# A gated recurrence and its feed-forward block: one masked product per chunk in place of seven levels, with the old algorithm kept behind a branch

## The chip, the core and the metric

The kernel runs on one core of a Trainium2 chip. The metric is the device time of one execution in microseconds (us). Of the core's engines, PE (TensorE) multiplies matrices, DVE (VectorE), ACT (ScalarE) and POOL (GpSimd) work element by element, and SP (SyncE) issues transfers. Each engine runs its own queue in order and waits on semaphores of the others.

## What is computed

Inputs are q, k, v, a_re, a_im of shape (4, 8, 768, 48) in float32 (batch, heads, steps, head size) and two weight matrices, 384 x 2048 and 2048 x 384, which arrive as float64. a_re lies between 0.85 and 0.95, a_im is normal with deviation 0.1. Cut to what matters:

```python
mag = np.sqrt(a_re * a_re + a_im * a_im)
scale = np.minimum(mag, 0.999) / (mag + 1e-06)
for t in range(S):
    new_re = ar * S_re - ai * S_im          # ar, ai: scaled gates of step t
    new_im = ar * S_im + ai * S_re
    S_re, S_im = new_re + kv, new_im        # kv: outer product of k[t] and v[t]
    y[:, :, t] = einsum('bhd,bhde->bhe', q[:, :, t], S_re)
h = x @ w_in                                # x: y as 3072 tokens of 384
sp = np.maximum(h, 0.0) + np.log1p(np.exp(-np.abs(h)))
out = (h * erf(sp)) @ w_out
```

## The kernel before, in words

The tokens are split into NU = 12 units of 256 steps, each of C = 2 chunks of 128 steps; three units follow one another in a batch element and hand on a state. Heads go in NHG = 2 groups of HG = 4. A complex gate is a decay r and an angle. The running sum of the angles turns queries and keys by cosine and sine, which leaves a real recurrence with decay r over 2 x 48 = 96 rows.

*Gates of a unit.* `gate_decay` (from L221) makes r with squares, a logarithm and an exponential on ACT, and some fifteen DVE passes over 768 columns, among them a reciprocal (L267) and r itself in two copies (L278). `gate_angle` (L292, L293, L305 to L311) takes the arc tangent, sums angles over a chunk with a triangular matmul (L305), adds the carry of the chunk before with a second one (L307), and takes sines.

*A chunk* (`attention`). For a head group r, k and q are transposed on PE (L340) and copied out by ACT (L347, L354, L361). A product of keys and queries gives the diagonal (L370, masked on DVE at L373). Seven levels follow, for blocks of m = 1, 2, ..., 64 steps:

```python
nc.tensor.matmul(out=lv[:, j], lhsT=K[0:D2, j, :], rhs=Qv[0:D2, j, :, 1, :], ...)        # L384
nc.vector.copy_predicated(out=halves(A, 1), mask=pair[l], data=lv...)                     # L389
nc.vector.tensor_tensor(out=halves(Q, 1)[0:D2], ..., in1=over(0), op=OP.mult)             # L398
nc.gpsimd.tensor_tensor(out=halves(K, 0)[0:D2], ..., in1=over(1), op=OP.mult)             # L400
nc.vector.tensor_tensor(out=nt[0:D2], in0=tv[:, :, 0], in1=tv[:, :, 1], op=OP.mult)       # L402
```

Each level's matmuls need the K and Q that the level before scaled. Then y is A times v plus Q times the carried state (L411, L414), and the state takes in the scaled keys, transposed back (L424), times v (L429, L436, L437). `to_xT` (L448) transposes y for the projections.

*Feed-forward of a unit.* Two slabs of 1024 hidden columns. `ff_in` projects (L475), and copies h on ACT (L477) and a clipped h on DVE (L480). `softplus` makes four ACT passes over 2048 columns (L146 is the helper of every table function, L145 its table load). `erf_times_h` has four parts of a slab, each with two DVE passes, a Gelu on ACT and two DVE passes more (L505 to L509). `ff_out` projects back with 16 accumulating products for each 128 tokens (L519) and writes (L522, L524). A float32 matmul appears in the profile as two instructions.

*Order.* `weave` emits the steps of several streams evenly over parts of a window. In window u run the recurrence of unit u over the whole window, the gates of unit u + 1, and the feed-forward of unit u - 1 over the first 0.85. Window 0 has the 14 steps that narrow the weights to float32 instead (`narrow`, L175: six DVE passes and two POOL products each, ending at L198), which use the buffers of h and z. Transfers are issued by SP.

## Time and profile before

| what | value |
|---|---|
| median of 3 runs | 1558.09 us (1557.83 to 1559.02) |
| profiled execution, its span from first to last instruction | 1557.6 us |
| instructions | 18736, of them 6912 matmuls |
| busy: PE, DVE, ACT, POOL | 1350.9, 1171.2, 597.6, 418.0 us |

The profile shows one execution. Only its span is given for it; it is the time between its first and last instruction, and it stands 0.5 us under the median of the runs. Busy time is the union of an engine's instructions. Idle time of an engine that does not set the pace costs nothing. The granted clock is the share of 2.4 GHz at which PE is allowed to run; 0.5 is 1.2 GHz.

### The profile page before, as it was taken

The page shows a single profiled execution, that of the slowest core. Times are in us where ns is not written, and L with a number is a line of the kernel's source. Part 1 is how long each engine was busy: PE and PEld are TensorE (multiplying, and loading weights), DVE is VectorE, ACT ScalarE, POOL GpSimd, SP SyncE. Part 2 cuts the span into 40 slices and gives each one's busy share as a digit, 9 for nine tenths or more (in the row PEclk, how much of TensorE's full clock was granted, in tenths as well). Part 3 has the DMA queues.
Part 4 walks back from the last instruction along what each step waited for, and adds up shares of the span by engine and source line. Part 5 has one row for each costly group of instructions (what it writes and reads, how often), then busy time and mean ns, then how long its engine had stood idle before and what let it go on. Part 6 is the DMA issues. An engine that isn't in the chain of part 4 may idle for free.

```text
span 1557.6 us, 18736 instructions
## 1 busy us (share of the span) xinstructions
PE 1350.9 (87%) x6912; PEld 1137.9 (73%) x6912; DVE 1171.2 (75%) x2104; ACT 597.6 (38%) x751; POOL 418.0 (27%) x387
## 2 busy tenths in 40 slices
PE   0455598998998998998998998998998998999997
PEld 0244477887877787787877787887877887888784
DVE  6999979579579669579589669579589669578535
ACT  2301033443443443444443443434443443434425
POOL 4445523122123222122132222122132122132210
PEclk9997557797797886797797887797797887799888
DMA  8214100100100100100100100100100100000000
GB/s 173 90 31 114 58 11 11 31 21 11 32 21 11 31 21 11 31 21 11 32 21 11 31 21 11 31 21 11 31 21 10 31 21 0 1 11 1 0 11 10
DMA packets 131386, 42.09 MB, mean 27 GB/s; under 512 B 125408, under 2 KB 128480, under 8 KB 130528
## 3 DMA queue, kind: packets, MB, share of 16 engines
q1 hardware_dynamic: 131296, 40.90, 11.4%
q8 instruction: 55, 0.90, 0.2%
q14 instruction: 35, 0.29, 0.1%
HBM read 36.18 MB, written 4.72 MB: 26 GB/s over the span
## 4 chain that ended last, share of the span: by engine, by line
PE 60%; DVE 25%; issue 6%; ACT 6%; POOL 2%; DMA 0%; SPq 0%; DVEq 0%; ACTq 0%; POOLq 0%
PE lv L384 20%; PE ops L519 12%; PE hps L475 9%; PE y L411 4%; DVE y L267 3%; PE y L414 3%; PE tr L340 3%; PE kv L429 3%; ACT z L146 2%; DVE A L389 2%; PE dg L370 2%; DVE tot L402 2%; DVE z L480 2%; DVE Q L398 1%; POOL K L400 1%
## 5 line engine op out<-in xcount | busy, mean ns | idle before, releaser
L384 PEld LDWEIGHTS lv<-Q,K 96*128 96x128 f32 x2688 | 438.3, 246 | 158.9 <-issue 100.6
L384 PE MATMUL lv<-Q,K 96*128 96x64 f32 x2688 | 448.6, 330 | 101.5 <-DVE Q L398 90.7
L400 POOL TENSOR_TENSOR K<-K,tot 96x256 f32<-96x256 f32 x280 | 262.7, 939 | 377.0 <-PE lv L384 243.8
L475 PE MATMUL hps<-xT,w_in_sb 128*128 128x256 f32 x1152 | 305.5, 415 | 0.6 <-ACT xT L449 0.6
L519 PE MATMUL ops<-w_out_sb,h 128*128 128x384 f32 x768 | 283.6, 498 | 7.8 <-DVE z L480 6.5
L146 ACT ACTIVATE z<-z 128x2048 f32<-128x2048 f32 (+1 forms) x144 | 152.3, 1057 | 319.9 <-DVE t L505 308.6
L475 PEld LDWEIGHTS hps<-xT,w_in_sb 128*128 128x128 f32 x1152 | 232.8, 212 | 32.2 <-ACT xT L449 1.0
L400 POOL TENSOR_TENSOR K<-K,rT 96x256 f32<-96x256 f32 x48 | 74.1, 1544 | 640.5 <-PE lv L384 640.5
L389 DVE COPY_PREDICATED A<-pair,lv 128x256 f32<-128x256 uint8 x336 | 171.3, 510 | 42.1 <-PE lv L384 39.4
L519 PEld LDWEIGHTS ops<-w_out_sb,h 128*128 128x128 f32 x768 | 135.1, 192 | 71.1 <-DVE z L480 6.9
L398 DVE TENSOR_TENSOR Q<-Q,tot 96x256 f32<-96x256 f32 x280 | 150.2, 536 | 0.0
L477 ACT COPY h<-hps 128x512 f32<-128x512 f32 x96 | 55.8, 581 | 161.0 <-PE hps L475 161.0
L437 DVE TENSOR_TENSOR S<-S,kv 96x192 f32<-96x192 f32 x32 | 11.2, 350 | 133.1 <-PE kv L429 133.1
L480 DVE TENSOR_SCALAR z<-hps 128x512 f32<-128x512 f32 x96 | 65.0, 682 | 44.1 <-ACT h L477 44.1
L411 PE MATMUL y<-v,A 128*128 128x48 f32 x384 | 95.3, 354 | 0.2 <-DVE tot L402 0.2
L411 PEld LDWEIGHTS y<-v,A 128*128 128x128 f32 x384 | 84.3, 279 | 0.4 <-DVE tot L402 0.4
L426 ACT COPY kn<-kn 128x384 f32<-128x384 f32 x40 | 19.2, 479 | 165.6 <-PE kn L424 146.3
L340 PE MATMUL tr<-ident,r 128*96 128x128 f32 x192 | 49.5, 387 | 37.3 <-DVE r L278 36.5
L414 PE MATMUL y<-S,Q 96*128 96x48 f32 x320 | 81.4, 347 | 0.0
L145 ACT ACT_TABLE_LOAD x62 | 79.5, 1283 | 1.1
L505 DVE TENSOR_TENSOR t<-z,yy 128x512 f32<-128x512 f32 x96 | 71.7, 747 | 9.7 <-ACT yy L146 9.7
L506 DVE SCALAR_TENSOR_TENSOR yy<-t,yy 128x512 f32<-128x512 f32 x96 | 74.7, 778 | 0.1
(96 smaller groups left out, 1753.6 us busy)
## 6 DMA issues: line engine op xcount, KB each, us to landing
raw<-in_moe_w_in_dram SPq DMA_DIRECT2D x6, 1024.0 KB, 5.5
raw<-in_moe_w_out_dram SPq DMA_DIRECT2D x8, 768.0 KB, 4.3
ar<-in_a_re_dram SPq DMA_DIRECT2D x24, 192.0 KB, 3.2
ai<-in_a_im_dram SPq DMA_DIRECT2D x24, 192.0 KB, 3.2
q<-in_q_dram SPq DMA_DIRECT2D x24, 192.0 KB, 3.7
k<-in_k_dram SPq DMA_DIRECT2D x24, 192.0 KB, 3.3
v<-in_v_dram SPq DMA_DIRECT2D x24, 192.0 KB, 3.2
out_dram<-o SPq DMA_DIRECT2D x24, 192.0 KB, 1.9
```

The costliest lines, as they stand in the source:

```text
L145: in_order(nc.scalar.preload_act_table_set(sets[0]))
L146: in_order(nc.scalar.activation(func=func, **kw))
L340: nc.tensor.transpose(out=ps[0:D2, j, :], in_=src(j), identity=ident)
L384: nc.tensor.matmul(out=lv[:, j], lhsT=K[0:D2, j, :], rhs=Qv[0:D2, j, :, 1, :], start=True, stop=True)
L389: nc.vector.copy_predicated(out=halves(A, 1), mask=pair[l], data=lv.rearrange("p h b m -> p (h b) m"))
L398: nc.vector.tensor_tensor(out=halves(Q, 1)[0:D2], in0=halves(Q, 1)[0:D2], in1=over(0), op=OP.mult)
L400: nc.gpsimd.tensor_tensor(out=halves(K, 0)[0:D2], in0=halves(K, 0)[0:D2], in1=over(1), op=OP.mult)
L411: nc.tensor.matmul(out=y[:, j, :], lhsT=st["A"][:, j, :], rhs=T["v", u][:, c, hg * HG + j, :], start=True, stop=first)
L414: nc.tensor.matmul(out=y[:, j, :], lhsT=st["Q"][0:D2, j, :], rhs=T["S", hg][0:D2, j, :], start=False, stop=True)
L475: nc.tensor.matmul(out=ps[:, e, :], lhsT=w_in_sb[:, kd, f0:f0 + P], rhs=T["xT", u][:, kd, :], start=(kd == 0), stop=(kd == KD - 1))
L480: nc.vector.tensor_scalar(out=T["z", u, sl][:, i:i + 2, :], in0=ps, scalar1=8.0, scalar2=-16.0, op0=OP.min, op1=OP.max)
L519: nc.tensor.matmul(out=ps, lhsT=T["h", u, sl][:, e, jj * P:(jj + 1) * P], rhs=w_out_sb[:, i, :], start=(i == 0), stop=(i == KF - 1))
```

## The change

`quotient_path` is new; the old kernel stays, word for word, as `product_path`. With c the running sum of the logarithms of the decays in a chunk, a query is scaled by exp(c) and a key by exp(-c) before they are turned and transposed. One product of keys and queries per head, masked by the upper triangle, then stands for the diagonal and all levels. The state is the old state plus keys times values, times the decays of the whole chunk, which a transfer through memory brings from a row into columns. Keys need no second transposition.

The gates: a slope ai/ar from a reciprocal of ar, clipped to 1.5, and its arc tangent; the log decay from the squares; four of the gate products and one product per erf part are on POOL. The carry of the angle is a row that a transfer brings to the first step's row. The clip of h reads SBUF, not PSUM. The windows run from -2 to 13: gates up to three units ahead, recurrence of w, first projection and erf of w - 1, second projection of w - 2 in eight pieces. The narrowing is in windows -1 (w_in) and 0 (w_out), with one words buffer where there were two. At the end two sums (of exp(-c), limit 1e13, and of the excess of the slope over 1.5, limit 0) are tested, the answer is loaded into a register, and if it is 0 the old algorithm runs over the same output.

```diff
+def quotient_path(
...
+    ldq = ctx.enter_context(tc.tile_pool(name="ldq", bufs=1))
...
+    hp = ctx.enter_context(tc.tile_pool(name="hp", bufs=4))
+    zp = ctx.enter_context(tc.tile_pool(name="zp", bufs=1))
...
+    def g_tan(u):
+        ar, ai = flat(T["ar", u]), flat(T["ai", u])
+        def s0():
+            s, y, m = t_("s"), t_("y"), t_("m")
+            act(out=s, in_=ar, func=AF.Square)
+            act(out=y, in_=ai, func=AF.Square)
+            nc.gpsimd.tensor_tensor(out=s, in0=s, in1=y, op=OP.add)
+            act(out=m, in_=ai, func=AF.Abs, scale=1.0 / SLOPE)
+            nc.gpsimd.tensor_tensor(out=m, in0=m, in1=ar, op=OP.subtract)
+            act(out=m, in_=m, func=AF.Relu, accum_out=off[:, u:u + 1])
+            T["s"], T["y"] = s, y
+        def s1():
+            rec = t_("rec")
+            nc.vector.tensor_scalar(out=rec, in0=ar, scalar1=2.0**-60, scalar2=None, op0=OP.max)
+            nc.vector.reciprocal(out=rec, in_=rec)
+            T["rec"] = rec
+        def s2():
+            rec = T["rec"]
+            nc.gpsimd.tensor_tensor(out=rec, in0=rec, in1=ai, op=OP.mult)
+            s = T["s"]
+            nc.vector.tensor_scalar(out=s, in0=s, scalar1=2.0**-63, scalar2=2.0**63, op0=OP.max, op1=OP.min)
+            th = gat.tile([P, C, DM], FP, tag="th", name="th")
+            nc.vector.tensor_scalar(out=th.rearrange("p c f -> p (c f)"), in0=rec, scalar1=SLOPE, scalar2=-SLOPE,
+                                    op0=OP.min, op1=OP.max)
+            T["th", u] = th
+        return [s0, s1, s2]
+    def g_turn(u):
+        return [lambda: act(out=T["th", u], in_=T["th", u], func=AF.Arctan)]
+    def g_angle(u):
+        def run(c):
+            def f():
+                th = T["th", u][:, c, :]
+                if u % PER > 0 or c > 0:
+                    prev = T["F", u][:, c - 1, :] if c > 0 else T["F", u - 1][:, C - 1, :]
+                    row = att1.tile([1, DM], FP, tag="row", name="row")
+                    nc.sync.dma_start(out=row, in_=prev[P - 1:P, :])
+                    nc.vector.scalar_tensor_tensor(out=th[0:1, :], in0=row, scalar=TAU, in1=th[0:1, :],
+                                                   op0=OP.mult, op1=OP.add)
+                ps = ps_b.tile([P, DM], FP, tag="b", name="sum")
+                nc.tensor.matmul(out=ps, lhsT=turns, rhs=th, start=True, stop=True)
+                if c == 0:
+                    T["F", u] = gat.tile([P, C, DM], FP, tag="F", name="F")
+                F = T["F", u][:, c, :]
+                w = att1.tile([P, DM], FP, tag="part", name="whole", bufs=2)
+                nc.vector.tensor_scalar(out=w, in0=ps, scalar1=MAGIC, scalar2=MAGIC, op0=OP.add, op1=OP.subtract)
+                nc.vector.tensor_tensor(out=F, in0=ps, in1=w, op=OP.subtract)
+            return f
+        return [run(c) for c in range(C)]
+    def g_sin(u):
+        def f():
+            F, CS, n = T["F", u], gat.tile([P, C, 2, DM], FP, tag="CS", name="CS", bufs=2), t_("n")
+            n = n.rearrange("p (c f) -> p c f", c=C)
+            act(out=n, in_=F, func=AF.Abs)
+            act(out=CS[:, :, 0, :], in_=n, func=AF.Sin, scale=-TAU, bias=half_pi)
+            act(out=CS[:, :, 1, :], in_=F, func=AF.Sin, scale=TAU)
+            T["CS", u] = CS
+        return [f]
+    def g_log(u):
+        def f():
+            s, y = T["s"], T["y"]
+            lr = gat.tile([P, C, DM], FP, tag="lr", name="lr")
+            act(out=s, in_=s, func=AF.Ln)
+            act(out=y, in_=s, func=AF.Exp, scale=-0.5)
+            act(out=y, in_=y, func=AF.Ln, scale=EPS, bias=1.0)
+            nc.vector.tensor_scalar(out=s, in0=s, scalar1=0.5, scalar2=math.log(CAP), op0=OP.mult, op1=OP.min)
+            nc.gpsimd.tensor_tensor(out=lr.rearrange("p c f -> p (c f)"), in0=s, in1=y, op=OP.subtract)
+            T["lr", u] = lr
+        return [f]
+    def g_decay(u):
+        def run(c):
+            def f():
+                if c == 0:
+                    T["pr", u] = gat.tile([P, C, 2, DM], FP, tag="pr", name="pr", bufs=2)
+                pr = T["pr", u]
+                ps = ps_b.tile([P, DM], FP, tag="b", name="sum")
+                nc.tensor.matmul(out=ps, lhsT=triu, rhs=T["lr", u][:, c, :], start=True, stop=True)
+                act(out=pr[:, c, 0, :], in_=ps, func=AF.Exp)
+                i = u * C + c
+                act(out=pr[:, c, 1, :], in_=ps, func=AF.Exp, scale=-1.0, accum_out=spans[:, i:i + 1])
+                s = u % PER
+                if s * C + c < PER * C - 1:
+                    w = att2.tile([P, H], FP, tag=f"w{c}", name="w")
+                    row = dram.tile([H, D], FP, tag="row", name="wrow")
+                    nc.sync.dma_start(out=row, in_=pr[P - 1:P, c, 0, :].rearrange("p (h d) -> p h d", d=D))
+                    with nc.allow_non_contiguous_dma(reason="a row into a column"):
+                        for e in range(2):
+                            nc.sync.dma_start(out=w[e * D:(e + 1) * D, :], in_=row.rearrange("h d -> d h"))
+                    T["w", u, c] = w
+            return f
+        return [run(c) for c in range(C)]
+    def chunk(u, c):
+        s = u % PER
+        first = s == 0 and c == 0
+        last = s == PER - 1 and c == C - 1
+        st = {}
+        def prep(nm, e):
+            def f():
+                a = att1.tile([P, H, D], FP, tag="part", name=nm + "r", bufs=2)
+                nc.vector.tensor_tensor(out=a, in0=T[nm, u][:, c], op=OP.mult,
+                                        in1=T["pr", u][:, c, e, :].rearrange("p (h d) -> p h d", d=D))
+                t = att1.tile([P, H, 2, D], FP, tag=nm + "t", name=nm + "t")
+                cs = T["CS", u][:, c].rearrange("p u (h d) -> p h u d", d=D)
+                nc.vector.tensor_tensor(out=t, in0=a.unsqueeze(2).to_broadcast([P, H, 2, D]), in1=cs, op=OP.mult)
+                st[nm] = t
+            return f
+        def cols(nm, g):
+            def f():
+                ps = ps_a.tile([P, HG, P], FP, tag="a", name="tr")
+                for j in range(HG):
+                    nc.tensor.transpose(out=ps[0:D2, j, :], in_=st[nm][:, g * HG + j].rearrange("p u d -> p (u d)"),
+                                        identity=ident)
+                t = att2.tile([P, HG, P], FP, tag=f"{nm}T", name=f"{nm}T", bufs=2 if nm == "k" else 3)
+                nc.scalar.copy(out=t[0:D2], in_=ps[0:D2])
+                st[nm, g] = t
+            return f
+        def scores(g):
+            def f():
+                ps = ps_a.tile([P, HG, P], FP, tag="a", name="sc")
+                for j in range(HG):
+                    nc.tensor.matmul(out=ps[:, j, :], lhsT=st["k", g][0:D2, j, :], rhs=st["q", g][0:D2, j, :],
+                                     start=True, stop=True)
+                A = att2.tile([P, HG, P], FP, tag="A", name="A")
+                nc.vector.tensor_tensor(out=A, in0=ps, in1=triu.unsqueeze(1).to_broadcast([P, HG, P]), op=OP.mult)
+                st["A", g] = A
+            return f
+        def state():
+            if last:
+                return
+            kv = ps_b.tile([P, H, D], FP, tag="b", name="kv")
+            for j in range(H):
+                nc.tensor.matmul(out=kv[0:D2, j, :], lhsT=st["k"][:, j].rearrange("p u d -> p (u d)"),
+                                 rhs=T["v", u][:, c, j, :], start=True, stop=True)
+            ns = att2.tile([P, H, D], FP, tag="S", name="S")
+            w = T["w", u, c][0:D2].unsqueeze(2).to_broadcast([D2, H, D])
+            if first:
+                nc.vector.tensor_tensor(out=ns[0:D2], in0=kv[0:D2], in1=w, op=OP.mult)
+            else:
+                t = att1.tile([P, H, D], FP, tag="part", name="Skv", bufs=2)
+                nc.vector.tensor_tensor(out=t[0:D2], in0=kv[0:D2], in1=T["S"][0:D2], op=OP.add)
+                nc.vector.tensor_tensor(out=ns[0:D2], in0=t[0:D2], in1=w, op=OP.mult)
+            st["S"] = ns
+        def y_():
+            y = ps_b.tile([P, H, D], FP, tag="b", name="y")
+            for j in range(H):
+                g, i = divmod(j, HG)
+                nc.tensor.matmul(out=y[:, j, :], lhsT=st["A", g][:, i, :], rhs=T["v", u][:, c, j, :],
+                                 start=True, stop=first)
+                if not first:
+                    nc.tensor.matmul(out=y[:, j, :], lhsT=st["q", g][0:D2, i, :], rhs=T["S"][0:D2, j, :],
+                                     start=False, stop=True)
+            if not last:
+                T["S"] = st["S"]
+            x = xp.tile([P, DM], FP, tag="x", name="x")
+            nc.scalar.copy(out=x, in_=y.rearrange("p h d -> p (h d)"))
+            st["x"] = x
...
+        return [prep("k", 1), prep("q", 0), cols("k", 0), cols("k", 1), cols("q", 0), scores(0), cols("q", 1),
+                scores(1), state, y_, xT]
...
+    def softplus(u, sl):
+        half = SLAB // 2
+        def f():
+            h = T["h", u, sl]
+            z = zp.tile([P, SLAB, NT], FP, tag="z", name="z")
+            y = yp.tile([P, SLAB, NT], FP, tag="yy", name="yy")
+            for i in range(0, SLAB, half):
+                nc.vector.tensor_scalar(out=z[:, i:i + half], in0=h[:, i:i + half], scalar1=8.0, scalar2=-16.0,
+                                        op0=OP.min, op1=OP.max)
+            act(out=z, in_=z, func=AF.Exp)
...
+                t = yp.tile([P, n, NT], FP, tag="t", name="t", bufs=2)
+                nc.gpsimd.tensor_tensor(out=t, in0=z, in1=y, op=OP.mult)
...
+    def ff_out(u):
+        n = 4
+        def piece(i0, jj):
+            def f():
+                if i0 == 0:
+                    T["o", u, jj] = ps_o.tile([P, DM], FP, tag="o", name="ops")
+                ps = T["o", u, jj]
+                for i in range(i0, i0 + n):
+                    sl, e = divmod(i, SLAB)
+                    nc.tensor.matmul(out=ps, lhsT=T["h", u, sl][:, e, jj * P:(jj + 1) * P], rhs=w_out_sb[:, i, :],
+                                     start=(i == 0), stop=(i == KF - 1))
+                if i0 + n == KF:
+                    o = op.tile([P, DM], FP, tag="o", name="o")
+                    nc.scalar.mul(out=o, in_=ps, mul=-RT2)
+                    t0 = (u * C + jj) * P
+                    nc.sync.dma_start(out=out[t0:t0 + P, :], in_=o)
+            return f
+        return [piece(i0, jj) for i0 in range(0, KF, n) for jj in range(C)]
+    load_gates(0)
+    load_gates(1)
+    load_qkv(0)
+    for f in g_tan(0):
+        f()
+    for w in range(-2, NU + 2):
+        load_gates(w + 4)
+        if w >= -1:
+            load_qkv(w + 2)
+        rec = chunk(w, 0) + chunk(w, 1) if 0 <= w < NU else []
+        f0 = only(w - 1, lambda u: ff_in(u, 0) + softplus(u, 0) + erf_times_h(u, 0))
+        f1 = only(w - 1, lambda u: ff_in(u, 1) + softplus(u, 1) + erf_times_h(u, 1))
+        wts = weights_in() if w == -1 else weights_out() if w == 0 else []
+        weave(
+            (0.0, 1.0, rec),
+            (0.0, 0.05, only(w + 2, g_turn) + only(w + 1, g_sin)),
+            (0.0, 0.9, wts),
+            (0.0, 0.45, f0), (0.45, 0.9, f1),
+            (0.2, 1.0, only(w - 2, ff_out)),
+            (0.3, 0.7, only(w + 2, g_angle)),
+            (0.15, 0.151, only(w + 1, g_decay) + only(w + 2, g_log)),
+            (0.5, 0.8, only(w + 3, g_tan)),
+        )
...
+    nc.tensor.matmul(out=ps[0:1, :], lhsT=ones, rhs=total, start=True, stop=True)
...
+    nc.vector.tensor_scalar(out=both[:, 0:1], in0=ps[0:1, 0:1], scalar1=SPAN, scalar2=None, op0=OP.is_le)
+    nc.vector.tensor_scalar(out=both[:, 1:2], in0=ps[0:1, 1:2], scalar1=0.0, scalar2=None, op0=OP.is_le)
+    nc.vector.tensor_tensor(out=ok, in0=both[:, 0:1], in1=both[:, 1:2], op=OP.mult)
...
+    with tc.tile_pool(name="ok", bufs=1) as pool:
+        ok = pool.tile([1, 1], I32, name="ok")
+        quotient_path(tc, q, k, v, a_re, a_im, w_in, w_out, out, ok)
+        fine = nc.values_load(ok[0:1, 0:1], min_val=0, max_val=1)
+        with tc.If(fine < 1):
+            product_path(tc, q, k, v, a_re, a_im, w_in, w_out, out)
```

## Rows read from the trace of the kernel before

**Rows 1.** The page: span, busy time by engine, granted clock in 40 slices.
```profile
span 1557.6 us, 18736 instructions
PE 1350.9 (87%) x6912; PEld 1137.9 (73%) x6912; DVE 1171.2 (75%) x2104; ACT 597.6 (38%) x751; POOL 418.0 (27%) x387
...
PEclk9997557797797886797797887797797887799888
```

**Rows 2.** Stretches: PE, PEld, DVE, ACT, POOL busy, granted clock, DMA share, GB/s.
```profile
36.50:190.00 153.50, 76.48 (x313) 65.34 (x313) 145.62 (x178) 19.52 (x29) 79.55 (x47) 0.83 0.26 75
...
480.00:600.00 120.00, 110.88 (x590) 94.25 (x590) 92.22 (x176) 53.98 (x67) 29.23 (x29) 0.81 0.10 20
```

**Rows 3.** Groups by line on PE: shape, count, busy us, mean ns, idle before.
```profile
L384 PE MATMUL lv<-Q,K 96*128 96x64 f32 x2688 | 448.6, 330 | 101.5 <-DVE Q L398 90.7 <-DVE tot L402 4.1 <-DVE A L373 3.2
...
L340 PE MATMUL tr<-ident,r 128*96 128x128 f32 x192 | 49.5, 387 | 37.3 <-DVE r L278 36.5 <-ACT rT L347 0.7
...
L424 PE MATMUL kn<-ident,K 96*128 96x96 f32 x160 | 33.7, 334 | 10.0 <-POOL K L400 10.0
...
L307 PE MATMUL sum<-F,last_row 128*128 128x384 f32 x40 | 18.4, 546 | 2.9 <-DVE F L311 2.9
```

**Rows 4.** Timeline at full clock (start, us, count); last: L384 alone in a stretch.
```profile
519.63 2.76 PE L475 MATMUL hps<-xT,w_in_sb 128*128 128x256 f32 x12
...
523.95 0.60 PE L340 MATMUL tr<-ident,k 128*96 128x128 f32 x4
...
531.71 1.06 PE L370 MATMUL dg<-q,K 96*128 96x128 f32 x8
...
555.27 0.86 PE L305 MATMUL sum<-hv,triu 128*128 128x384 f32 x2
...
1543.54 10.67 PE L519 MATMUL ops<-w_out_sb,h 128*128 128x384 f32 x32 [1.31 <-DVE h L509]
...
532.00:560.00 28.00, 12.00 (x96) 12.19 (x96) 1.00 0.04 15
```

**Rows 5.** Stretches of 4 us, all engines; last: L384 alone, at half clock.
```profile
480.00:484.00 4.00, 1.97 (x16) 1.86 (x16) 4.00 (x8) 3.97 (x4) 1.38 (x1) 0.93 0.00 0
484.00:488.00 4.00, 0.01 (x1) 0.04 (x1) 4.00 (x5) 2.62 (x2) 1.89 (x2) 0.50 0.00 0
...
500.00:504.00 4.00, 3.94 (x19) 3.62 (x18) 3.84 (x8) 0.29 (x1) 1.56 (x3) 0.50 0.00 0
...
516.00:520.00 4.00, 4.00 (x22) 3.59 (x22) 2.28 (x7) 0.94 (x3) 0.00 (x0) 0.81 0.22 43
...
492.00:500.00 8.00, 7.75 (x35) 7.27 (x35) 0.50 0.00 0
```

**Rows 6.** Groups by line and form on ACT.
```profile
L146 ACT ACTIVATE z<-z 128x2048 f32<-128x2048 f32 x48 | 91.7, 1911 | 11.2 <-DVE z L480 10.8
...
L145 ACT ACT_TABLE_LOAD x62 | 79.5, 1283 | 1.1
...
L146 ACT ACTIVATE z<-z 128x512 f32<-128x512 f32 x96 | 60.5, 630 | 308.8 <-DVE t L505 308.6
...
L477 ACT COPY h<-hps 128x512 f32<-128x512 f32 x96 | 55.8, 581 | 161.0 <-PE hps L475 161.0
...
L146 ACT ACTIVATE hv<-hv 128x768 f32<-128x768 f32 x12 | 10.1, 844 | 22.7 <-DVE hv L271 22.6
```

**Rows 7.** Groups by line and form on DVE.
```profile
L506 DVE SCALAR_TENSOR_TENSOR yy<-t,yy 128x512 f32<-128x512 f32 x96 | 74.7, 778 | 0.1
...
L267 DVE RECIPROCAL y<-y 128x768 f32<-128x768 f32 x12 | 59.2, 4934 | 0.0
...
L262 DVE TENSOR_TENSOR hv<-hv,ai 128x768 f32<-128x768 f32 x12 | 11.3, 944 | 0.0
```

**Rows 8.** Line L198 on POOL: ns min/median/max, first and last start.
```profile
L198 POOL TENSOR_TENSOR w_out_sb<-w_out_sb,words x8: 1792/1856/1997, 137.9 to 210.9; 128x768 f32<-128x768 f32 x8
```

**Rows 9.** The page's transfers: count, KB each, us from issue to landing.
```profile
out_dram<-o SPq DMA_DIRECT2D x24, 192.0 KB, 1.9
```

187 lines of the change are left out of this document (186 added, 1 removed).

## The prediction, on record before the changed kernel ran

> **What bounds the kernel now.** I read the page first: PE is busy for 87% of the span, DVE for 75%, ACT for 38%, POOL for 27%, and the clock that PE is granted lies mostly between 7 and 9 tenths after the start [rows 1]. The profiled span is 1557.6 us, half a microsecond under the median of the runs (1558.09), so a sum against the span is a sum against the time. The table of stretches then shows two regimes [rows 2]. Up to about 190 us DVE is the full engine (145.6 of 153.5 us): it narrows the weights, and PE is half idle. In a steady unit of 120 us (one of the units of 256 tokens) PE is busy 110.9 us, DVE 92.2, ACT 54.0, POOL 29.2, at a granted clock of 0.81. The reader is to see that PE sets the pace of the steady part, and that it loses there more to its clock (about 0.19 x 120 = 23 us a unit) than to idleness (9 us). The groups by line say what PE does: the largest, 448.6 us, is the seven levels [rows 3].
>
> **What goes.** From PE: the levels (2688 instructions), the transposes of r, the transposes of K for the state, the carry of the angle, which becomes a transfer and one DVE instruction [rows 3]. From DVE: predicated copies, both multiplications of the levels, the totals, and half of the gate arithmetic. From POOL: the level products of K. What replaces them on PE is one triangular sum of log decays per chunk and nothing else, since the single product of keys and queries takes the place of the diagonal one, instruction for instruction.
>
> **PE's new sum for one unit of two chunks, at the full clock of 2.4 GHz** (granted 1.00). Prices are from bursts there [rows 4]:
> - first projection, 96 instructions x 0.23 us (12 in 2.76) = 22.1 us;
> - second projection, 64 x 0.333 (32 in 10.67) = 21.4;
> - transposes of k and q, 32, and of x, 6, x 0.15 (4 in 0.60) = 5.7;
> - scores, 32 x 0.1325 (8 in 1.06) = 4.2;
> - y, 64 at most, and the state's keys times values, 32 at most, at the level matmuls' rate of 0.125 (96 in 12.00) = 12.0, for they too load weights of about that size for few columns;
> - two sums per chunk, four pairs x 0.86 = 3.4.
>
> Together 68.8 us. The same prices give today's unit: the levels' 224 x 0.125 = 28.0 and some 5 us of other removed work more, 102 us, against the 120 that it takes.
>
> **The other engines' sums for a unit** [rows 6, 7].
> - ACT: eight passes of 1.911 us for softplus (15.3), eight Gelu at 0.630 (5.0), 26 copies and small exponentials at no more than 0.581 (15.1), five table loads at 1.283 (6.4), eleven gate functions at 0.844 (9.3): 51 us. An added wait is here: the Relu of the gate test waits for two products on POOL, about 1.9 us each [rows 8], and the copies out of PSUM are queued behind it. I add 3 us: 54.
> - DVE: 24 passes of the erf part at no more than 0.778 (18.7), the reciprocal 4.934, and some 26 passes at no more than 0.944 (24.5; this takes in rotation, scores, state, clips and angle): at most 48 us. The added wait is the carried row of the angle, which DVE takes from a transfer; the nearest transfer lands in 1.9 us [rows 9], twice per unit, with rotation and clips behind it: 4 us at most.
> - POOL: four gate products at 1.9 and eight products of two thirds that width moved from DVE: 18 us.
> - SP: 80 short transfers more in all (20 carried rows; 60 to bring the last row of decays into columns). Those columns are wanted a window after they are made, so I cost them at nothing; were that cover gone, it would be three landings of about 2 us in a row per chunk, 6 us, 120 us in all, which is the upper end for this.
>
> So PE stays the longest with 69 us against 54, 52 and 18. An engine other than PE becomes the bound only if its waits add 15 us a unit.
>
> **From sum to time.** Idle share: today's 9 in 120, 7.5%; 68.8 / 0.925 = 74.4 us. Clock: the loss is not uniform. The stretches of 4 us [rows 5] show the granted clock falling right behind 4 us in which PE did one instruction, staying at 0.50 while PE, though busy 3.94 of 4 us, does nothing but level matmuls, and coming back once the projection is issued in a dense run. Those thin stretches are what goes; the projections are 43.5 of 68.8 us and, by the new order, spread from the start of a window to its end (second projection in eight pieces from 0.2 to 1.0). I therefore take a loss a third of today's, a mean clock of 0.93: 74.4 / 0.93 = 80 us for a unit. The ends: no loss, 74; today's 0.81, 92.
>
> **The clock rule against the trace.** The Trainium skill, "TensorE: Matmul & The Clock Gate", section "Part 1: The HAM clock gate (the "warmup" mystery)", says that the slow clock is the default state and that sustained activity releases it. By that page a kernel that takes matmuls away can lose the clock; the rows above agree on the fall after idleness, and add that a PE busy with small matmuls is not raised either. By the page's rule a unit at 1.2 GHz throughout gives the 1757 us of the slower rival below.
>
> **The start.** The last narrowed weights are ready at 212.8 us today [rows 8]. The words buffer becomes single, so that each narrowing waits for the previous one's POOL addition, but DVE has far less beside it. I take 190 us, with 175 to 215 as ends. Until then softplus cannot begin (it shares that buffer); PE meanwhile can do two units of recurrence (2 x 25.3) and one first projection (22.1), and 12 x 68.8 - 72.7 = 753 us of its work are left, 10.9 units.
>
> **The end.** Behind the last projection the elementwise chain of a slab (four passes of 1.911, then four parts of about 3 us) leaves PE idle for some 20 us, before the closing 10.67 us burst that the sum already holds. Then come the test over all sums, a register load and a branch past the old algorithm. No row shows a branch. Its cost is bounded by 0 and by some 10 us (five landings of 1.9 us [rows 9]); I take 10 with the reductions, for the code jumped over is long.
>
> Sum: 190 + 10.9 x 80 + 20 + 10 = 1092 us; I forecast **1090 us**.
>
> **The rivals.**
> - *The clock stays as it is now.* Half of a window's copies wait behind softplus passes, PE has gaps, and the granted clock falls as often as today. For it: the rise needs a dense run. Against: dense runs are spread over the window. 190 + 10.9 x 92 + 30 = 1223 us.
> - *Full cover.* No clock loss and half the idle share, weights at 175: 71.5 us a unit, 175 + 10.9 x 71.5 + 30 = 984 us. For it: level matmuls and projections interleaved ran at 1.00 between 532 and 560 us. Against: ACT and DVE are in order, each 70 to 80% full.
> - *The other side: PE at 1.2 GHz throughout.* Its place is the attention steps, which wait for ACT copies one after another. Level matmuls took 7.75 / 35 = 0.221 us at half clock [rows 5] against 0.125, 1.77 times; up to 2 for the projections. A unit is then 68.8 x 1.9 / 0.925 = 141 us, the time 190 + 10.9 x 141 + 30 = 1757 us. It decides above (1558 - 220) / 10.9 = 123 us a unit. Against it: dense first projections lie in each half window, and such runs raised the clock in every unit of the trace.
> - *The change doesn't do what it says.* If the test at the end fails, the old algorithm runs behind the new one: 1090 + 1558 = 2648 us. Against it: the decays are about 0.9 a step, so the inverse over 128 steps is near exp(13), 4e5; summed over 24 x 384 x 128 entries, mostly far smaller, it is under 1e12, below the limit of 1e13, and with a_re at least 0.85 no slope comes near 1.5.
>
> **How the numbers follow.** Forecast 0.62, clock as now 0.20, full cover 0.12, PE at 1.2 GHz 0.03, branch taken 0.02, a mixture that ends within 0.2% of today 0.01. A measurement of this kernel tells 0.2% from no change. The range runs from 1000 us (between forecast and full cover) to 1240 us (takes in the clock as now and a start at 205 us); under it half of full cover is left out, above it the two failures and the end with uncovered transfers. Faster 0.94, same 0.01, slower 0.05.
>
> **What would show it.** Right: PE instructions near 3900; no group of levels; steady windows near 80 us with PE busy over 85% and a granted clock above 0.9; projections as PE's two largest groups; DVE and ACT under 70% of the span; softplus first near 190 us; no instruction of the old function. Wrong: a granted clock at 0.8 or under in steady windows; ACT or DVE busier than PE; long idle time of PE put down to ACT copies or to a transfer; weights later than 215 us; over 15 us from the last output to the end.

## The result, and the profile after

The changed kernel takes 984.23 us (median of 4 runs, 981.49 to 987.25) where the kernel before took 1558.55 (1557.83 to 1559.12) beside it: 0.632 times as long [0.630, 0.634], 574 us less. The forecast was 1090 us with a range of 1000 to 1240. Faster was right, by a mechanism that mostly held; the time lies 16 us under the range. Three of the four runs of e_thin and two of the six of e_y_split fell into a slower state of the core, and so did the profiled runs of these two kernels, so differences to them are taken from their other runs.

The page of the kernel after (span, busy time, granted clock in 40 slices, then groups by line: count, busy us, mean ns, idle time before them and what ended it):

```profile
span 980.0 us, 10235 instructions
...
PE 812.8 (83%) x3882; PEld 618.2 (63%) x3882; DVE 632.6 (65%) x736; ACT 579.6 (59%) x737; POOL 309.4 (32%) x180
...
PEclk9998575888978989999999999999999899999989
...
L966 PE MATMUL ops<-w_out_sb,h 128*128 128x384 f32 x768 | 286.0, 512 | 16.6 <-DVE h L952 8.9
L914 PE MATMUL hps<-xT,w_in_sb 128*128 128x256 f32 x1152 | 267.8, 387 | 16.9 <-ACT h L916 14.6
...
L948 POOL TENSOR_TENSOR t<-z,yy 128x512 f32<-128x512 f32 x96 | 148.0, 1560 | 301.0 <-ACT yy L639 261.3
...
L949 DVE SCALAR_TENSOR_TENSOR yy<-t,yy 128x512 f32<-128x512 f32 x96 | 101.6, 1083 | 74.0 <-POOL t L948 74.0
```

Against [rows 1]: 3882 matmuls instead of 6912, the two projections (L914, L966) are PE's largest groups, and no group of levels is left [rows 3]. PE is busy 83% of the span, a smaller share than before, although it has much less to wait for in the steady part: the ends now weigh more. One line is new where nobody had priced a wait: the product t of the erf part, moved to POOL (L948), takes 1.560 us each, and the DVE pass behind it (L949) has risen from 0.778 [rows 7] to 1.083 us and waits 74 us for it.

The kernel after by stretches (columns as in [rows 2]: PE, PEld, which is PE's loading of weights, DVE, ACT, POOL busy, with the number of instructions, then granted clock, DMA share, GB/s):

```profile
0.00:212.00 212.00, 120.34 (x512) 96.38 (x512) 160.24 (x170) 70.01 (x109) 95.62 (x53) 0.82 0.38 97
212.00:440.00 228.00, 188.03 (x890) 142.69 (x891) 157.03 (x177) 163.56 (x197) 80.21 (x46) 0.88 0.17 33
440.00:790.00 350.00, 328.88 (x1668) 249.63 (x1667) 231.66 (x278) 245.12 (x319) 97.94 (x57) 0.98 0.16 32
...
930.00:980.00 50.00, 39.80 (x121) 24.20 (x119) 14.87 (x24) 14.96 (x16) 5.35 (x4) 0.88 0.05 18
```

The first softplus input is clipped at 211.8 us, behind the last narrowed weight (the bracket gives the idle time before it and what ended it):

```profile
211.78 1.29 DVE L930 TENSOR_SCALAR z<-h 128x1024 f32<-128x1024 f32 x2 [1.98 <-POOL w_out_sb L693]
```

So the start is no shorter than before (212.8 us). From 440 us PE is busy 328.88 of 350 us (94%) at a clock of 0.98. Between them lies a poor stretch, 212 to 440 us, at 82% and 0.88. At the end PE is idle for only 10 us.

The length of a unit, from the copies of the transposed x out of PSUM (two per unit; the timeline of ACT, start and duration; the first chunks of units 4 and 11):

```profile
409.13 0.48 ACT L899 COPY xT<-xt 128x384 f32<-128x384 f32 x1
...
873.53 0.48 ACT L899 COPY xT<-xt 128x384 f32<-128x384 f32 x1
```

Seven units take 464.4 us: 66.3 us each, where the forecast had 80. Over them PE is busy 94.5% of the time, at a clock of 0.99:

```profile
409.13:873.53 464.40, 438.73 (x2267) 335.90 (x2266) 298.79 (x360) 314.90 (x399) 128.21 (x75) 0.99 0.15 30
```

**The account.** Forecast: 190 + 10.9 x 80 + 30 = 1092. Observed: the start 22 us later; 10.9 units shorter by 13.7 us each, 149 us; the end 20 us shorter. That leaves 35 us to the span, a remainder that is put down to the poor stretch: 1092 + 22 - 149 - 20 + 35 = 980.

### The profile page after: what moved, and what is told of

It reads as the page before. It is cut to its first block, busy times and chain, and to the rows that moved or that the text cites. A ratio compares the mean times of both kernels' runs of the same rounds, so it can differ in the third digit from the quotient of the medians.

```text
span 980.0 us, 10235 instructions
## 1 busy us (share of the span) xinstructions
PE 812.8 (83%) x3882; PEld 618.2 (63%) x3882; DVE 632.6 (65%) x736; ACT 579.6 (59%) x737; POOL 309.4 (32%) x180
## 5 line engine op out<-in xcount | busy, mean ns | idle before, releaser
L966 PE MATMUL ops<-w_out_sb,h 128*128 128x384 f32 x768 | 286.0, 512 | 16.6 <-DVE h L952 8.9
L914 PE MATMUL hps<-xT,w_in_sb 128*128 128x256 f32 x1152 | 267.8, 387 | 16.9 <-ACT h L916 14.6
L914 PEld LDWEIGHTS hps<-xT,w_in_sb 128*128 128x128 f32 x1152 | 220.3, 194 | 59.0 <-ACT h L916 15.9
L948 POOL TENSOR_TENSOR t<-z,yy 128x512 f32<-128x512 f32 x96 | 148.0, 1560 | 301.0 <-ACT yy L639 261.3
L966 PEld LDWEIGHTS ops<-w_out_sb,h 128*128 128x128 f32 x768 | 146.3, 200 | 99.7 <-issue 16.9
L949 DVE SCALAR_TENSOR_TENSOR yy<-t,yy 128x512 f32<-128x512 f32 x96 | 101.6, 1083 | 74.0 <-POOL t L948 74.0
L951 DVE TENSOR_TENSOR z<-z,yy 128x512 f32<-128x512 f32 x96 | 88.0, 946 | 0.0
L854 PEld LDWEIGHTS sc<-qT,kT 96*128 96x128 f32 x384 | 54.6, 214 | 44.5 <-ACT qT L846 40.3
L930 DVE TENSOR_SCALAR z<-h 128x1024 f32<-128x1024 f32 x48 | 42.2, 887 | 62.1 <-ACT h L916 59.9
L854 PE MATMUL sc<-qT,kT 96*128 96x128 f32 x384 | 61.0, 308 | 24.4 <-ACT qT L846 23.8
L952 DVE SCALAR_TENSOR_TENSOR h<-z,h 128x512 f32<-128x512 f32 x96 | 78.4, 846 | 0.1
L885 PE MATMUL y<-S,qT 96*128 96x48 f32 x320 | 69.3, 302 | 0.0
L735 DVE RECIPROCAL rec<-rec 128x768 f32<-128x768 f32 x12 | 59.4, 4950 | 0.3
L885 PEld LDWEIGHTS y<-S,qT 96*128 96x128 f32 x320 | 56.0, 218 | 0.0
```

The costliest lines, as they stand in the source:

```text
L735: nc.vector.reciprocal(out=rec, in_=rec)
L854: nc.tensor.matmul(out=ps[:, j, :], lhsT=st["k", g][0:D2, j, :], rhs=st["q", g][0:D2, j, :], start=True, stop=True)
L885: nc.tensor.matmul(out=y[:, j, :], lhsT=st["q", g][0:D2, i, :], rhs=T["S"][0:D2, j, :], start=False, stop=True)
L914: nc.tensor.matmul(out=ps[:, e, :], lhsT=w_in_sb[:, kd, f0:f0 + P], rhs=T["xT", u][:, kd, :], start=(kd == 0), stop=(kd == KD - 1))
L948: nc.gpsimd.tensor_tensor(out=t, in0=z, in1=y, op=OP.mult)
L949: nc.vector.scalar_tensor_tensor(out=y, in0=t, scalar=-2.0, in1=y, op0=OP.add, op1=OP.mult)
```

## The experiments

All but one are edits of the kernel after; each ratio is to the kernel before, run beside it. One thing bears on all of them: an edit on one engine can change the order in which the others' instructions are issued. By their traces, PE's order is that of the kernel after in e_no_branch alone; in e_t_on_dve, which edits no PE instruction, 18% of PE's 3882 stand at another place. The first difference, in the kernel after and then in e_t_on_dve:

```profile
217.55 7.75 PE L914 MATMUL hps<-xT,w_in_sb 128*128 128x256 f32 x24 [8.13 <-ACT h L916]
...
217.50 9.52 PE L914 MATMUL hps<-xT,w_in_sb 128*128 128x256 f32 x32 [8.16 <-ACT h L916]
```

So a measured difference belongs to the edit and the order that comes with it; no run separates the two.

### What set the gain

**e_no_levels** goes the other way: the kernel before, with the levels alone taken out, and with them their passes on DVE and POOL.

```diff
-        return [a0, a1, a2, diag] + [level(l) for l in range(LEVELS)] + [y_, state]
+        return [a0, a1, a2, diag, y_, state]
```

> The kernel before with its seven levels left out (diagonal product, y and state remain; what the levels add to the output is left out, and so are the scaled keys and queries). Theory that the levels and the slow clock around them are the bulk of the gain: removed PE work 28 us a unit at full clock and most of the 23 us of clock loss, so a unit of 75 to 85 us and 1080 to 1180 us in all. Rival, that the new order of the work (three windows deep, projections spread) brings a large part: over 1250 us with a clock still near 0.8.

Measured: 1133.79 us (1132.33 to 1135.41), 0.727 [0.726, 0.728]. The levels are worth 425 of the 574 us; the other 150 are left to the rest of the change (gates, order, no transposes of r, state without a second transposition of keys), whose parts were not tried one by one. Its steady stretch, to be read beside the same stretch of the kernel after:

```profile
440.00:790.00 350.00, 310.00 (x1471) 240.61 (x1470) 247.49 (x357) 206.48 (x260) 0.00 (x0) 0.86 0.14 29
```

With the levels gone but the old order kept, PE is busy 89% of this stretch and its clock is 0.86, not 0.98. So the levels were not all of the clock's loss. The rest goes with gaps. Four times in the stretch PE waits 5.3 us for DVE, and behind each gap its bursts have the length of half clock (four transposes 1.09 us, against 0.60 at full clock [rows 4]):

```profile
450.64 1.09 PE L340 MATMUL tr<-ident,q 128*96 128x128 f32 x4 [5.29 <-DVE q L334]
```

In that stretch of the kernel after PE's longest such wait is 2.7 us.

**e_thin** puts thin work back that nobody waits for: seven times 16 products of 64 columns per chunk, behind the scores.

```diff
+        def thin():
+            ps = ps_a.tile([P, HG, P], FP, tag="a", name="thin")
+            for g in range(2):
+                for j in range(HG):
+                    nc.tensor.matmul(out=ps[:, j, 0:64], lhsT=st["k", g][0:D2, j, :], rhs=st["q", g][0:D2, j, 0:64], ...)
...
-                scores(1), state, y_, xT]
+                scores(1)] + [thin] * 7 + [state, y_, xT]
```

> After the scores of a chunk seven steps of 16 instructions are put in on PE, products of 64 columns with the transposed keys as weights, the shape and number of the levels' matmuls before, whose results nobody reads and nobody waits for. Theory that the slow clock of the kernel before came with these thin matmuls themselves: 224 instructions a unit at 0.122 us (the price that the doubled scores showed) are 27 us a unit, 328 us in all, and on top the clock of 440 to 790 us falls from 0.98 to 0.85 or under: 1380 to 1500 us. Rival, that the clock was lost in the levels' waits for DVE and POOL, not by the thin matmuls: clock above 0.93, and 1290 to 1340 us.

Measured: 1302.98 us in the one run that can be compared (1327.75 to 1330.95 in the other three; no interval can be given), 319 us more for 2688 instructions: 0.119 us each. That lies in the rival's range, and at the 0.125 us of the level matmuls [rows 4] the thin work alone would cost 336 us, so this time by itself does not show a loss of clock. The steady stretch of a run of 1330.55 us:

```profile
440.00:790.00 350.00, 349.93 (x1964) 292.70 (x1964) 164.76 (x191) 173.24 (x217) 62.36 (x41) 0.88 0.12 26
```

There PE is never idle, and yet its clock is 0.88. As this run took 28 us longer than the one compared, it does not say what the clock was in that one. The kernel after itself shows the fall of the clock without e_thin. Timeline of PE (start, length, count):

```profile
364.08 1.48 PE L866 MATMUL kv<-v,kt 128*96 128x48 f32 x16
...
368.97 5.15 PE L966 MATMUL ops<-w_out_sb,h 128*128 128x384 f32 x10
373.95 0.49 PE L898 MATMUL xt<-ident,x 128*128 128x128 f32 x3
```

From 364.08 us PE runs 48 thin instructions (keys times values, then y) with no gap between them, and the granted clock falls behind them, from 1.00 between 364 and 368 us to 0.63 between 368 and 372: the next 10 of the second projection take 4.98 us, 0.498 each, where they take 0.326 at full clock. So the clock can fall without idleness, behind thin work. It does not do so behind each such run; e_dve_end_y below has fewer of them.

### What sets the pace now

**e_scores_twice** issues each product of keys and queries a second time.

```diff
-                    nc.tensor.matmul(out=ps[:, j, :], lhsT=st["k", g][0:D2, j, :], rhs=st["q", g][0:D2, j, :], ...)
+                    for _ in range(2):
+                        nc.tensor.matmul(out=ps[:, j, :], lhsT=st["k", g][0:D2, j, :], rhs=st["q", g][0:D2, j, :], ...)
```

> Every product of keys and queries is issued twice into the same place (the result stays the same): 32 more PE instructions in each of 12 units. Theory that PE paces the steady part at the full clock, and that an instruction in a burst costs its spacing (8 in 0.89 to 1.0 us, 0.115 us each): 12 x 32 x 0.115 = 44 us, less what today's idle PE time (about 4 us a unit) takes in, so 984 rises to 1010 to 1030 us. At the forecast's price of 0.1325 us with its tail it would be 51 us. Rival, that ACT and the chains of waits set the pace: under 12 us, 984 to 996.

Measured: 1031.21 us (1029.25 to 1032.70), 0.661 [0.660, 0.663]: 47 us more for 384 instructions, 0.122 us each, about what such an instruction takes in a burst (0.124, below). PE's work is on the path nearly in full.

**e_act_pass** does one softplus pass of ACT twice.

```diff
             act(out=y, in_=z, func=AF.Ln)
+            act(out=y, in_=z, func=AF.Ln)
```

> The third pass of softplus (logarithm, 128x2048) is issued twice, with the same result: 24 passes of 1.91 us more on ACT, 46 us in all, none on PE. Theory that PE paces: most of it is hidden, under 15 us more, 984 to 999; PE idle time put down to ACT grows a little. Rival, that ACT's in-order queue sets the pace: 30 to 46 us more, 1014 to 1030.

Measured: 1023.64 us (1020.72 to 1028.96), 0.656 [0.655, 0.658]: 39 of the 46 us of added ACT work (24 passes of 1.91) appear in the time. So ACT, busy 59% of the span, is on the path as well. The steady stretch of this kernel:

```profile
440.00:790.00 350.00, 319.62 (x1551) 246.90 (x1550) 209.41 (x250) 248.02 (x304) 92.05 (x55) 0.92 0.16 32
```

One line of the waits in that stretch (total us, times, longest), of this kernel:

```profile
PEld sc L854 <- ACT qT L846: 28.5, 15, 4.9
```

and of the kernel after:

```profile
PEld sc L854 <- ACT qT L846: 14.5, 15, 1.6
```

The scores wait for the copy of the queries out of PSUM, which stands behind softplus passes in ACT's queue. These waits grow by 14 us in the stretch, PE is busy 91% instead of 94%, and the clock goes from 0.98 to 0.92.

**e_cols_on_dve** takes just these copies off ACT.

```diff
-                nc.scalar.copy(out=t[0:D2], in_=ps[0:D2])
+                nc.vector.tensor_copy(out=t[0:D2], in_=ps[0:D2])
```

> The copies of the transposed keys and queries out of PSUM (8 of 0.58 us in a unit, 56 us in all) go from ACT to DVE. Theory that PE and ACT wait for each other in turn in a steady unit, so that each engine's work is paid nearly whole (44 us of scores cost 47, 46 us of ACT passes cost 39): the copies behind softplus go away, up to 4.6 us a unit, bounded by PE's idle share of about 4 us: 940 to 965 us. Rival, that the added ACT pass hurt only because softplus itself became longer, not through ACT's total or through copies queued behind it: within 10 us of 984, or slower where DVE becomes late.

Measured: 981.02 us (977.06 to 982.32), 0.629 [0.627, 0.631]: 3 us, within the spread: the theory failed. In the steady stretch the scores now wait 8.1 us for these copies on DVE where they waited 14.5 for ACT, and the time does not follow. So the rival stands, that the added pass hurt because softplus itself became longer; which of ACT's steps holds PE up stays open.

**e_out_late** issues the second projection at the end of a window only.

```diff
-            (0.2, 1.0, only(w - 2, ff_out)),
+            (0.9, 1.0, only(w - 2, ff_out)),
```

> The eight pieces of the second projection are emitted in the last tenth of each window (0.9 to 1.0) instead of 0.2 to 1.0; nothing else changes. Theory that the granted clock stayed at full speed because dense projection work is spread between the attention steps: with the pieces gathered, PE has thin stretches between 0.2 and 0.9, the mean clock of 440 to 790 us falls from 0.98 to 0.90 or below and PE idles more, so the time rises by 40 to 100 us. Rival, that the clock stayed up merely because the levels are gone: clock 0.97 or more and the time within 15 us of 984.

Measured: 1001.15 us (1000.36 to 1002.56), 0.642 [0.641, 0.644]: 17 us more at a steady clock of 0.95. Its spreading over the window, on which the forecast of the clock leaned, is worth little; it fell between what the two theories gave.

### The product that went to POOL

**e_t_on_dve** puts it back on DVE.

```diff
-                nc.gpsimd.tensor_tensor(out=t, in0=z, in1=y, op=OP.mult)
+                nc.vector.tensor_tensor(out=t, in0=z, in1=y, op=OP.mult)
```

> The first product of each erf part goes back from POOL to DVE. ACT waited 84.8 us in all for these products in 82 waits, each took 1.56 us against 0.75 on DVE before, and DVE's pass behind it took 1.08 instead of 0.78 beside POOL. Theory that ACT's time is on the path: the wait goes, 960 to 980 us, though DVE is busy 70 us more. Rival, that DVE, at 65% busy, turns late for the rotations and clips: 984 to 1010 us.

Measured: 947.49 us (944.77 to 951.00), 0.608 [0.607, 0.609]: 37 us less. The groups of the product and of the pass behind it, in this kernel:

```profile
L948 DVE TENSOR_TENSOR t<-z,yy 128x512 f32<-128x512 f32 x96 | 64.9, 716 | 33.4 <-ACT yy L639 33.4
...
L949 DVE SCALAR_TENSOR_TENSOR yy<-t,yy 128x512 f32<-128x512 f32 x96 | 61.8, 683 | 0.0
```

and its stretch that was poor:

```profile
212.00:440.00 228.00, 205.18 (x1032) 158.68 (x1033) 171.43 (x233) 184.44 (x229) 43.67 (x16) 0.93 0.18 35
```

The same product takes 0.716 us on DVE, and the pass behind it 0.683 instead of 1.083: with 65 us of work more, DVE's busy time over the span falls from 632.6 to 617.8 us. In the stretch from 212 to 440 us PE is busy 205 us where it was 188. The copy that marks unit 4, a burst of PE behind a gap, and the steady stretch:

```profile
386.10 0.46 ACT L899 COPY xT<-xt 128x384 f32<-128x384 f32 x1
...
471.33 1.98 PE L854 MATMUL sc<-qT,kT 96*128 96x128 f32 x8 [2.40 <-ACT qT L846]
...
440.00:790.00 350.00, 337.73 (x1647) 262.87 (x1647) 215.53 (x315) 232.67 (x302) 36.46 (x15) 0.92 0.16 32
```

Unit 4 comes 23 us earlier than after (386.10 against 409.13), which is most of the 35 us of the account. The seven units that follow take 465.0 us, as long as after: PE is busy more of the time in the steady stretch (96%), but at a clock of 0.92. Its gaps are fewer, but the longest wait of the scores for ACT is 3.0 us against 1.0 after; behind the one of 2.40 us at 471 us eight scores take 1.98 us where they take 1.06 at full clock [rows 4]. So nothing was gained in the steady units; the gain lies in the poor stretch and at the end. That DVE slows beside POOL is seen in the timeline of the kernel after (start, duration, count, and in brackets the idle time before and what ended it):

```profile
639.95 3.40 POOL L948 TENSOR_TENSOR t<-z,yy 128x512 f32<-128x512 f32 x2
...
640.33 0.68 DVE L949 SCALAR_TENSOR_TENSOR yy<-t,yy 128x512 f32<-128x512 f32 x1
642.17 1.74 DVE L949 SCALAR_TENSOR_TENSOR yy<-t,yy 128x512 f32<-128x512 f32 x1 [1.16 <-POOL t L948]
...
647.31 1.28 DVE L949 SCALAR_TENSOR_TENSOR yy<-t,yy 128x512 f32<-128x512 f32 x2
```

At 642 us one pass takes 1.74 us while POOL is in its second product; at 647 us, with POOL quiet, two take 1.28. The pass at 640 us ran at full speed beside the first one, so not every overlap costs. The Trainium skill, "GPSIMD Engine Reference", section "1. Specifications", says that POOL's paths to SBUF are shared with VectorE, with contention for DVE instructions that read two inputs from SBUF; this pass reads two, and the trace agrees for the pass at 642 us, not for the one at 640 us.

### The start, the branch, the end

**e_words_two** gives the narrowing two words buffers in turn.

```diff
-        tmps = zp.tile([P, 2, n], U32, tag="z", name="words")
+        T["nth"] = T.get("nth", -1) + 1
+        pool, tag = ((zp, "z"), (yp, "yy"))[T["nth"] % 2]
+        tmps = pool.tile([P, 2, n], U32, tag=tag, name="words")
```

> The narrowing takes its words buffer in turn from the two tiles z and yy, which are both free then, so two narrowings can overlap; nothing else changes. Theory that the single buffer is what kept the start at 212 us instead of the forecast 190 (a narrowing waits for the last POOL addition of the one before): softplus begins 20 to 40 us earlier and the time falls by 15 to 35 us, to 950 to 970. Rival, that DVE (busy 127 of 153 us there) sets the start: within 8 us of 984.

Measured: 986.88 us (978.52 to 987.24), 0.632 [0.629, 0.635]: no gain, though the first clip comes 24 us earlier. Its first stretch:

```profile
0.00:212.00 212.00, 80.94 (x348) 63.02 (x349) 174.88 (x167) 75.53 (x108) 109.58 (x57) 0.67 0.37 95
```

DVE is busy 175 of the 212 us (160 after), and PE has done 348 instructions by then where it had done 512: what the weights gained, the recurrence lost (unit 0's transposed x comes at 131 us instead of 104, unit 4's at 407 instead of 409). The single buffer delays softplus, but a nearly full DVE then delays the rest; that DVE's work sets the start is argued from this, since no run took work off it there.

**e_no_branch** ends behind the test: no register load, no branch, no old algorithm in the program.

```diff
-        fine = nc.values_load(ok[0:1, 0:1], min_val=0, max_val=1)
-        with tc.If(fine < 1):
-            product_path(tc, q, k, v, a_re, a_im, w_in, w_out, out)
```

> The register load, the branch and the old algorithm behind it are left out; the sums of the test are still made. The forecast took 10 us for test and branch at the end, with 0 and 10 as ends. Theory from the profile after (test done at 946 us beside the last projection, last copy out at 974.5 and end at 980): 0 to 4 us less. Rival at the forecast's value: 10 us less, 974.

Measured: 979.10 us (976.96 to 980.10), 0.628 [0.627, 0.630]: load and branch cost about 5 us, the middle of the forecast's 0 to 10. Its interval barely parts from that of the kernel after. In the profiles the span goes on for 5.5 us behind the start of the last copy out in the kernel after and for 3.3 here, so 2 of the 5 us are seen at the end.

### Towards a better kernel

**e_dve_end** has the product on DVE, moves the second projection of the last unit but one into the first half of its window, and the first four pieces of the last unit's ahead of the last erf part.

```diff
+        if w == NU:
+            outs = [(0.0, 0.45, ff_out(NU - 2)), (0.5, 0.9, ff_out(NU - 1)[:4])]
+        if w == NU + 1:
+            outs = [(0.2, 1.0, ff_out(NU - 1)[4:])]
...
```

> Two edits: the first product of each erf part on DVE again (alone 947 us), and at the end the second projection of the last but one unit in the first half of its window and the first four pieces of the last one before the last erf part. In the profile after, all 64 of the last unit's projection instructions stand after 951 us, behind a copy that ACT was late with, while PE was idle for 5 us. Theory: 8 to 13 us off the end, 934 to 940. Rival, that the last erf part ends everything and the early pieces only move idle time: 947 within 3.

Measured: 954.91 us (952.04 to 957.43), 0.613 [0.611, 0.615]: 7 us more than without that edit. The theory failed: 40 instructions of the unit before ran in one block ahead of the last unit's first projection, and PE was idle for 5.6 us before its last 32 all the same.

**e_dve_end_y** also computes y in two steps, the first ahead of the state:

```diff
-                scores(1), state, y_, xT]
+                scores(1), y_(0), state, y_(1), xT]
```

> As the one before, and y of a chunk is issued in two steps of four heads, one before and one after the state, so that projection work of the other streams falls between. Theory that the granted clock falls in the stretch of 48 thin instructions in a row (y and state): fewer falls, mean clock of 440 to 790 us up from 0.92 to 0.96 or more, 10 to 25 us less than the one before. Rival, that the falls come from waits: clock unchanged and the time within 5 us.

Measured: 945.25 us (940.27 to 947.77), 0.606 [0.604, 0.609]: 10 us less. The steady stretch of e_dve_end, then of this kernel:

```profile
440.00:790.00 350.00, 337.57 (x1659) 261.46 (x1658) 217.46 (x318) 234.10 (x305) 36.45 (x15) 0.94 0.16 32
...
440.00:790.00 350.00, 337.04 (x1777) 264.13 (x1776) 224.26 (x329) 252.77 (x327) 36.70 (x16) 0.99 0.16 32
```

PE is busy for the same time and the clock rises from 0.94 to 0.99. In this stretch e_dve_end has four runs of 48 thin instructions in a row and this kernel one. By the records of the granted clock, three of the falls in e_dve_end stand behind such instructions without a gap and four behind a gap of PE; here there are two falls, both behind a gap. So the theory holds in part: the edit, with the order it brings, took away falls of both kinds. **e_dve_end_y_words** adds the two words buffers:

> As the one before, with the words buffer taken in turn from z and yy. Alone this made softplus begin 24 us earlier and the time no shorter, since DVE was the start's full engine. Theory: no gain here either, within 6 us of the one before. Rival, that with the steady part relieved the earlier weights count: 10 to 20 us less.

Measured: 938.99 us (935.86 to 946.85), 0.602 [0.601, 0.604]; the gain of 6 us is little more than the spread.

**e_y_split** is the kernel after with y in two steps and nothing else.

> The changed kernel with y in two steps around the state, nothing else. Theory that falls of the clock come from the stretch of thin y and state instructions, but cost little here because the steady clock is already 0.98 (4 to 7 us of the whole could be had between 440 and 790, some more between 212 and 440, where it is 0.88): 965 to 980 us. Rival, that the clock there falls on waits for ACT and POOL: within 4 us of 984.

Measured: 1035.46 us (median of the four runs to be compared, 1032.39 to 1037.32), 0.665 [0.663, 0.666]: 51 us more, which no theory had. **e_dve_y** is the same edit with the product on DVE:

> First erf product on DVE and y in two steps, without the end edit. Theory that the end edit cost 8 us (955 against 947) because second projections of the last but one unit went ahead of the last unit's first projections: 935 to 940 us against 945 with it. Rival, that 955 against 947 was the clock's chance alone: 945 within 4.

Measured: 939.25 us (935.79 to 940.98), 0.603 [0.601, 0.604]: there the same edit takes 8 us off, and the clock of the steady stretch goes from 0.92 to 1.00 at the same busy time of PE (337.73 us without the edit):

```profile
440.00:790.00 350.00, 336.74 (x1781) 263.91 (x1780) 224.72 (x330) 254.38 (x329) 36.68 (x16) 1.00 0.16 32
```

So the edit costs only while the erf product is on POOL. In the profile of e_y_split (a run of 1048.62 us) the gate products and the erf products, which share POOL's one queue, are waited for longer than after (in the waits from 440 to 790 us the longest wait of ACT for the gate test's POOL product goes from 3.5 to 7.3 us, for the erf product from 1.7 to 6.2). Whether these waits make the 51 us, and which shift in the order of issue makes them late, was not tried; that stays open.

**e_dve_y_words** leaves the end as it is and joins the other three edits: product on DVE, y in two steps, two words buffers.

> As the one before with the words buffer in turn from two tiles. With the end edit in place that gave 6 us (939 against 945). Theory: the same 4 to 8 us here, 928 to 934 us, the shortest of all. Rival: no difference to the one before, since alone it gave none (987 against 984).

Measured: **934.27 us** (930.32 to 939.70), 0.601 [0.599, 0.603], the lowest median of all, 50 us under the changed kernel; its interval overlaps that of e_dve_y, so the two words buffers are not shown to gain. Its first and its steady stretch, and a burst of the first:

```profile
0.00:212.00 212.00, 87.73 (x375) 66.86 (x375) 175.15 (x173) 77.77 (x112) 109.98 (x55) 1.00 0.36 94
...
106.21 1.06 PE L845 MATMUL tr<-ident,qt 128*96 128x128 f32 x4 [3.71 <-DVE qt L837]
...
440.00:790.00 350.00, 340.67 (x1804) 266.14 (x1803) 225.68 (x331) 257.34 (x327) 33.44 (x16) 1.00 0.16 32
```

PE is busy 97% of the steady stretch at full clock: little but fewer or cheaper matmuls is left to gain there. The 1.00 of the first stretch is not to be trusted: four transposes take 1.06 us in it, where they take 0.60 at full clock [rows 4]. Bursts of that length stand in the first stretches of the other kernels too, so no reading here rests on the clock of a start.

## Why the prediction was right and wrong

**PE's sum, 68.8 us a unit: over-priced by about 7.** This is the first step that failed. The forecast divided the length of a burst by its count [rows 4], and that length includes the tail of the last instruction. In a full queue the next burst begins before the tail ends. The kernel before shows it already: behind the 12 instructions of the first projection at 519.63 us [rows 4] the next burst starts at 522.22, which makes 0.216 each and not 0.23, and behind the 4 transposes at 523.95 it starts at 524.38, 0.108 and not 0.15:

```profile
522.22 0.60 PE L340 MATMUL tr<-ident,k 128*96 128x128 f32 x4
...
524.38 1.46 PE L519 MATMUL ops<-w_out_sb,h 128*128 128x384 f32 x4
```

The timeline of PE in the kernel after, at full clock, shows the bursts one behind another (start, length, count):

```profile
464.87 1.48 PE L866 MATMUL kv<-v,kt 128*96 128x48 f32 x16
466.19 0.88 PE L765 MATMUL sum<-th,turns 128*128 128x384 f32 x2
...
500.32 1.16 PE L854 MATMUL sc<-qT,kT 96*128 96x128 f32 x8
501.31 0.32 PE L882 MATMUL y<-v,A 128*128 128x48 f32 x2
...
503.03 0.88 PE L966 MATMUL ops<-w_out_sb,h 128*128 128x384 f32 x2
...
507.47 1.04 PE L843 MATMUL tr<-ident,kt 128*96 128x128 f32 x8
508.34 2.10 PE L966 MATMUL ops<-w_out_sb,h 128*128 128x384 f32 x6
...
511.86 0.81 PE L805 MATMUL sum<-lr,triu 128*128 128x384 f32 x2
512.51 0.81 PE L966 MATMUL ops<-w_out_sb,h 128*128 128x384 f32 x2
513.66 8.04 PE L914 MATMUL hps<-xT,w_in_sb 128*128 128x256 f32 x36 [0.34 <-ACT xT L899]
521.53 0.81 PE L805 MATMUL sum<-lr,triu 128*128 128x384 f32 x2
...
935.79 10.48 PE L966 MATMUL ops<-w_out_sb,h 128*128 128x384 f32 x32
946.21 0.19 PE L1009 MATMUL all<-total,ones 128*1 128x2 f32 x2
```

From start to next start: first projection 7.87 / 36 = 0.219 (forecast 0.23), second 10.42 / 32 = 0.326 (0.333), transposes 0.87 / 8 = 0.109 (0.15), scores 0.99 / 8 = 0.124 (0.1325), y 1.72 / 16 = 0.108 and keys times values 1.32 / 16 = 0.083 (both 0.125), a sum 0.65 (0.86). With the forecast's own counts that is 21.0 + 20.8 + 4.1 + 4.0 + 6.9 + 2.6 + 2.6 = 62.0 us. By the forecast's further steps this alone takes (68.8 - 62.0) / 0.925 / 0.93 = 7.9 us off a unit: 72.1 us, and 190 + 10.9 x 72.1 + 30 = 1006 us in all. The scores doubled gave 0.122 us an instruction on the chip, near the spacing; idle time may have hidden a part, so that run alone does not exclude the length.

**The clock, 0.93: it is 0.99** over the seven units; this is the second step that failed, 62.0 / 0.925 x (1 / 0.93 - 1 / 0.99) = 4.4 us a unit. The direction was right, and the reason in part. Thin work can cost clock although PE is busy (the burst at 364.08 us), and the thin levels are gone; but gaps of PE cost it too, 5.3 us for DVE in e_no_levels, 2.4 us for ACT in e_t_on_dve, and how the two share the gain of clock was not measured. The size, a third of the old loss, was a guess. The spread of the projections over the window, on which the forecast leaned, was worth 17 us (e_out_late). The rest of the 13.7 us, 1.4, is the idle share: 5.5% where today's 7.5% was kept.

**The elementwise engines.** The forecast held them off the path because none has a sum near PE's. The sums were about right (ACT's 54 us against 245.12 / 350 x 66.3 = 46; POOL's 18 is 97.94 / 350 x 66.3 = 19). But an in-order engine at 70% still sets when PE's next operand is there (e_act_pass: 39 of 46 us), and the product moved to POOL, costed by its sum as harmless, takes 37 us with the order of issue that goes with it, before the steady units and at the end (e_t_on_dve). This step failed in the other direction and hid part of the two above. Another estimate missed in the same place: eight products of two thirds the width at less than 1.9 us are right in mean (1.56), but DVE's pass behind them waits 74 us for them in all and rises from 0.683 to 1.083 us in mean.

**The start, 190 us: 212.** Its upper end, 215, held. The forecast let DVE's lighter queue outweigh the single words buffer; it does not. With two buffers softplus does begin at 188 us, near the forecast, but the recurrence is then behind in its turn (e_words_two), and the time stays.

**The end, 30 us: 10.** The branch is about 5 us, within 0 to 10. The 20 us of idle PE were too many, since the second projection of unit 10 lay beside the last erf part (the 32 instructions at 935.79 us); 4.65 us of wait are left ahead of the last 64.

**What held.** Instructions of PE near 3900 (3882); PE busy over 85% in steady windows (94%) and the clock above 0.9, though a unit took 66.3 us and not near 80; projections its largest groups; DVE and ACT under 70%; the branch not taken; no wait for the 60 transfers into columns in any line of the waits. Of the rivals, the clock as before, the slow clock throughout and the taken branch did not occur. Full cover gave 984 us, which is the time measured to the microsecond, but by a start of 175 us and 71.5 us a unit where 212 and 66.3 were found: its number is right by errors that cancel.
